# Sums of weights from the first down projection on, and seven products for four blocks of the second batch

## The chip, the cores and the metric

The kernel runs on one core of one Trainium2 chip. The metric is the device time of one execution in microseconds (us). Of the core's engines the page names PE (TensorE, matrix products), PEld (its weight loads), DVE (VectorE), ACT (ScalarE), POOL (GpSimd) and SP (SyncE, which only issues DMAs here). PE writes its results to eight banks of PSUM; ACT and DVE carry them from there to SBUF. Each engine works through its own queue in order, so an instruction that waits holds up everything queued behind it.

## What is computed

Attention in a causal window of 128 positions with a linear bias for each head, for 8 batches of 8 heads with 576 positions and 64 channels, and after it a bilinear layer on the 4608 tokens (512 channels, 1536 hidden units):

```python
scores = scale * np.matmul(q, k.transpose(0, 1, 3, 2))
mask = (rel >= 0) & (rel < window)
scores = np.where(mask, scores + bias[None], -1000000000.0)
attn = np.exp(scores - np.max(scores, axis=-1, keepdims=True))
attn = attn / (np.sum(attn, axis=-1, keepdims=True) + 1e-09)
x = np.matmul(attn, v)              # then laid out as (tokens, 512)
out = (x @ w_a) * (x @ w_b) @ w_out
```

All of it is float32. The kernel gets that accuracy on PE from pairs of float16 numbers: a value is split into a high part and a remainder, and a product is made of three float16 products (high by high, high by low, low by high).

## The kernel before, in words

The work goes by batch, 0 to 7. For each batch stand an **up** stage (both products with `w_a` and `w_b` and their elementwise product, giving the hidden tile `h`) and a **down** stage (the product with `w_out`). PE's queue is written out by hand from batch 1 on: `batch(b)` walks through `up` and then `down` and, at each step of these generators, lets `attention()` advance in proportion (`Pace.along`). So the attention of the next batch lies between the matmuls of this one. An item of `attention()` is one pair of heads; batch 1's up stage carries 2.85 items (from place 5.15 to 8), its down stage two, and every later up and down stage two each. The order on DVE, ACT and POOL is made by a scheduler from the order of the code and priorities; SP's is that of the code. In batch 0 the scheduler also places PE's instructions.

The hidden units are 12 blocks `f` of 128. For one block the tokens of a batch make two halves (`t`) and the 512 channels two halves, and there are two ways to make the block:

- **plain** (`first_up`, `up_plain`): 4 results of 12 matmuls, 48 matmuls of 128x288 in all. They read the four parts of `wup[:, f]` and the splits 0, 1, 2 and 7 (`B12`) of the tokens in `xs`. ACT copies two results (L867) and casts the product (L848); DVE makes two products (L869) and the remainder (L849).
- **fast** (`up_fast`): 7 results of 6 matmuls, 42 in all, after a scheme of Strassen's kind. It needs sums of the parts of the weights (three in `wsum[:, f]`, the fourth written over part 3 of `wup[:, f]`, so that the block cannot be plain afterwards) and sums of the parts of the tokens (splits 3 to 6 in `xs`). Carrying away is ACT L881, L893, L899, L848; DVE L888, L904, L909, L916, L849; POOL L911. Two blocks run beside each other in two lanes, after four steps in which the first lane runs alone. Two of a block's products add to the bank that ACT L881 has just copied from.

`ways` says for each batch which blocks are plain and which fast; plain blocks come first. The sums of the weights come from the generator `sums_of_weights`, `spread`: 25 steps, one for each block and half of the channels, the last only finishing. A step adds on POOL (L248 on 512 columns, L249 to L252 on 128 each), and a step later the result is split by two casts on ACT (L258) and two subtractions on DVE (L260). `quota` says in which steps of a stage how many of them are handed out. POOL's part is ordered behind the last `bias` (L365, the row of biases of an attention item), ACT's behind the last evacuation of a result. The space for the intermediate sums is the end of `wsum` for blocks 0 to 7 and the attention's rotating tile `t` for blocks 8 to 11.

The weights themselves are converted before, in `weights` (the last of it in batch 0's down stage, with L231 on ACT and L232 on DVE writing `wdn`). The tokens are split by `split_x(st, plain, fast)` when a batch's attention is done, which is in the down stage of the batch before: each split is a cast on ACT (L441) and a subtraction on DVE (L442); the fast way adds four subtractions on POOL (L455, L458, L460, L465), which write over the tokens in `v`. The next `v` is loaded by SP once that tile is free.

The lines that matter most, besides those that follow below:

```python
def split(n, src):
    act.copy(xs[:, n, 0, :, :], src)
    vec.tensor_tensor(out=xs[:, n, 1, :, :], in0=src, in1=xs[:, n, 0, :, :], op=ALU.subtract)

# split_x(st, plain, fast), in short
split(0, b11)
if plain:
    split(1, b21); split(2, b22); split(B12, b12)
if not fast:
    return
# then four subtractions on POOL, and splits 4, 6, 5, 3 (and 2, 1 where not plain)
```

Of the kernel before, what the change touches and what calls it, by code (L numbers as in the profile page):

```python
# [21 lines left out]
B, H, S, D = 8, 8, 576, 64  # L22
# [24 lines left out]
def attention_then_bilinear_ffn(ctx: ExitStack, tc: tile.TileContext, qT, kT, vP, w_a, w_b, w_out, rel, slopes2, outT):  # L47
# [392 lines left out]
# [4 lines that stand above are left out]
    def split_x(st, plain, fast):  # L444

        b11, b12, b21, b22 = (st.v[:, k:k + 2, t:t + HT] for k in (0, 2) for t in (0, HT))
        split(0, b11)
        if plain:
            split(1, b21)
            split(2, b22)  # L450
            split(B12, b12)
        if not fast:
            return
        yield
        pool.tensor_tensor(out=b11, in0=b12, in1=b11, op=ALU.subtract)  # L455
        if not plain:
            split(2, b22)
        pool.tensor_tensor(out=b12, in0=b22, in1=b12, op=ALU.subtract)  # L458
        split(4, b11)
        pool.tensor_tensor(out=b22, in0=b22, in1=b11, op=ALU.subtract)  # L460
        yield
        if not plain:
            split(1, b21)
        split(6, b12)
        pool.tensor_tensor(out=b21, in0=b21, in1=b22, op=ALU.subtract)  # L465
        yield
        split(5, b22)
        split(3, b21)
        yield
# [197 lines left out]
    def attention():  # L667
# [29 lines left out]
        st, prev = load_v(1), None  # L697
# [4 lines left out]
        for i in range(n + 1):  # L702
            b, p = 1 + i // NPAIR, i % NPAIR
# [6 lines left out]
            if p == 1 and b > 1:  # L710
                st = load_v(b)
# [44 lines left out]
            if prev and p == 0:  # L756
                states[b - 1] = st
                assert started["down"] == b - 2
                for k, _ in enumerate(split_x(st, b - 1 <= 3, b - 1 >= 2)):
                    yield i + (4.2 + 0.2 * k) / 7  # L760
            yield i + 5 / 7
            if o:
# [198 lines left out]
    def out_scale(st):  # L961

        oi = small.tile([P, 1], F32, tag="oi", name="oi")
        vec.tensor_scalar(out=oi, in0=st.g, scalar1=smin, scalar2=so, op0=ALU.mult, op1=ALU.mult)
        vec.tensor_scalar(out=oi, in0=oi, scalar1=st.sv, scalar2=st.sv, op0=ALU.mult, op1=ALU.mult)
        vec.reciprocal(oi, oi)
        return oi

    def weave(main, *sides):

        for n, _ in enumerate(main):
            for side, a, z, steps in sides:
                if a <= n < z:
                    for _ in range((n + 1 - a) * steps // (z - a) - (n - a) * steps // (z - a)):
                        next(side, None)
# [24 lines left out]
    weights = chain(up_weights(), down_weights())  # L1000
# [4 lines left out]
    h = hid.tile([P, NF, 2, 2, HT], F16, name="h")  # L1005
# [4 lines left out]


    every = list(range(NF))
    ways = [(every, [])] * 2 + [(every[6:], every[:6]), (every[10:], every[:10])] + [([], every)] * (B - 4)
    att = Pace(attention())
    spread = sums_of_weights()

    quota = [((), ()), (((8, 48, 9),), ((0, 48, 4),)), (((0, 24, 3),), ((0, 48, 5),)), ((), ((0, 48, 4),))] + [((), ())] * (B - 4)

    def first_batch():
        st = states[0]  # L1020
        weave(att.along(first_up(st, h), 49, 3.2), (weights, 0, 40, 50))
        weave(att.along(first_down(0, out_scale(st), h), 24, 5.15), (weights, 0, 12, 12))
        for _ in weights:
            pass

# [8 lines left out]
    with tc.manual_schedule(engines=SP):  # L1034
        first_batch()
# [45 lines left out]
```

## Time and profile before

| | |
|---|---|
| median of 3 runs | 991.28 us (991.03 to 994.67) |
| the profiled execution's own time | 989.81 us |
| its span, first to last instruction | 988.0 us |
| granted TensorE clock, mean | 0.995 |
| DVE, ACT, POOL busy | 669.0, 635.6, 255.3 us |
| DMA packets | 102.82 MB, mean 104 GB/s |

The profile's page shows one execution. A row of a group gives line, engine and operation, what it writes and reads with the shapes, how often, then the busy time and the mean ns of one, and last the idle time of the engine before it with what ended it. The view by stretches of time gives for each stretch its length, then for each engine the busy time with the number of its instructions, and last PE's granted clock and the DMA share. The view of one tile gives for each group the shortest, the median and the longest duration. Stretches are cut here where PE passes from one stage to the next by the timeline: batch 0's up and down stages begin at 55.9 and 153.5 us, batch 1's at 200.3 and 281.8, batch 2's at 324.1 and 400.0, batch 3's at 441.1 and 513.2, batch 4's at 554.8 and 626.4, batch 5's at 667.1 and 737.9; the last up and down stages begin at 887.4 and 949.3.

### The profile page before, as it was taken

The numbers are of one execution on the slowest core, as the hardware profiler recorded it, in microseconds if no ns is written. First come the engines' busy times: TensorE is split into PE (matmuls) and PEld (weight loads), VectorE is DVE, ScalarE is ACT, GpSimd is POOL, SyncE is SP. The second block draws the span as 40 slices with busy tenths as digits, with TensorE's granted clock in tenths as the row PEclk, the third lists the DMA queues.
The fourth block names the chain that finished last, engine by engine and source line by source line (L and its number), as shares of the span: only waits on it lengthen the run. The fifth ranks groups of instructions, "written<-read, shape, count | busy, mean of one in ns | idle before, by whom it ended". The sixth has DMA issues, their size and how long they took to land.

```text
span 988.0 us, 23867 instructions
## 1 busy us (share of the span) xinstructions
PE 962.1 (97%) x9339; PEld 748.9 (76%) x9339; DVE 669.0 (68%) x1867; ACT 635.6 (64%) x1729; POOL 255.3 (26%) x309
## 2 busy tenths in 40 slices
PE   7899999999999999999999999999999999999998
PEld 5567777677777777777777777777777777877776
DVE  5979998668688657777778677757776576514520
ACT  5977769667676667766767766777667766413321
POOL 1211122032546313541225222211232012311100
PEclk8999999999999999999999999999999999999999
DMA  8434753664337234463345362373245432200001
GB/s 333 168 126 172 231 154 67 151 158 92 80 74 183 68 69 87 107 172 75 68 92 121 120 118 65 87 191 84 59 84 117 133 74 38 55 34 5 1 13 36
DMA packets 148432, 102.82 MB, mean 104 GB/s; under 512 B 120032, under 2 KB 128352, under 8 KB 147296
## 3 DMA queue, kind: packets, MB, share of 16 engines
q1 hardware_dynamic: 138816, 91.77, 38.2%
q10 hardware_dynamic: 9504, 9.54, 3.0%
q8 instruction: 73, 1.20, 0.5%
q14 instruction: 39, 0.32, 0.1%
HBM read 48.33 MB, written 9.44 MB: 58 GB/s over the span
## 4 chain that ended last, share of the span: by engine, by line
PE 69%; DVE 12%; ACT 7%; DMA 7%; issue 3%; POOL 1%; SPq 0%; ACTq 0%; DVEq 0%
PE ch L856 19%; PE dn_ps L952 18%; PE p L856 14%; PE up_ps L856 9%; PE x_ps L507 4%; DMA v<-in_vP 4%; PE sc_ps L384 3%; DVE phl L406 2%; PE dn_ps L818 2%; ACT t L389 1%; DVE wsum L135 1%; DVE xs L442 1%; ACT phl L405 1%; DVE wsum L134 1%; DMA qk<-in_kT 1%
## 5 line engine op out<-in xcount | busy, mean ns | idle before, releaser
L856 PEld LDWEIGHTS <-wup 128*128 128x128 f16 x3072 | 296.3, 98 | 82.0 <-issue 5.7
L952 PE MATMUL dn_ps<-h,wdn 128*128 128x288 f16 x2016 | 254.4, 286 | 0.0
L952 PEld LDWEIGHTS <-wdn 128*128 128x128 f16 x2016 | 193.9, 98 | 52.0 <-issue 0.2
L856 PE MATMUL up_ps<-xs,wup 128*128 128x288 f16 x1536 | 194.6, 286 | 1.1 <-ACT rc L867 0.8
L856 PEld LDWEIGHTS <-wsum 128*128 128x128 f16 x1152 | 111.7, 98 | 32.0 <-issue 2.5
L911 POOL TENSOR_TENSOR rc<-rc,row 128x288 f32<-128x288 f32 x64 | 62.3, 974 | 279.8 <-DVE row L909 263.9
L389 ACT ACTIVATE t<-t,mn 128x192 f32<-128x192 f32 (+2 forms) x252 | 107.2, 427 | 24.5 <-DVE mn L388 24.4
L856 PE MATMUL ch<-xs,wup 128*128 128x288 f16 x768 | 115.0, 286 | 0.5 <-ACT row L893 0.5
L856 PE MATMUL p<-xs,wup 128*128 128x288 f16 x768 | 115.1, 286 | 0.0
L406 DVE SCALAR_TENSOR_TENSOR phl<-t,rin,phl 128x192 f16<-128x192 f32 (+2 forms) x252 | 104.6, 454 | 15.3 <-ACT phl L405 15.1
L856 PE MATMUL ch<-xs,wsum 128*128 128x288 f16 x768 | 111.5, 286 | 1.1 <-ACT rc L881 1.1
L848 ACT CAST h<-rc 128x576 f16<-128x576 f32 x96 | 64.1, 668 | 69.1 <-DVE rc L916 37.2
L405 ACT ACTIVATE phl<-t,rin 128x192 f16<-128x192 f32 (+2 forms) x252 | 88.9, 425 | 25.3 <-DMA pT<-phl 12.7
L849 DVE TENSOR_TENSOR h<-rc,h 128x576 f16<-128x576 f32 x90 | 69.5, 772 | 30.5 <-ACT h L848 29.7
L388 DVE CUSTOM_DVE_ANT_0 t<-sc_ps,bias,neg 128x192 f32<-128x192 f32 (+2 forms) x216 | 73.9, 389 | 7.6 <-PE sc_ps L384 7.5
L957 ACT ACTIVATE row<-dn_ps,oi 128x288 f32<-128x288 f32 x56 | 27.6, 493 | 55.9 <-PE dn_ps L952 55.9
L893 ACT ACTIVATE row<-ch,g 128x288 f32<-128x288 f32 x64 | 31.8, 497 | 48.9 <-PE ch L856 48.9
L442 DVE TENSOR_TENSOR xs<-v,xs 128x576 f16<-128x576 f32 x52 | 47.8, 935 | 21.4 <-ACT xs L441 21.3
L888 DVE TENSOR_TENSOR rc<-p,rc 128x288 f32<-128x288 f32 x64 | 29.1, 454 | 44.3 <-PE p L856 34.7
L365 POOL TENSOR_SCALAR bias<-rel_sb,ninv,sl_sb 128x192 f32<-128x192 f32 x24 | 20.0, 832 | 147.8 <-DVE mn L388 129.8
L856 PE MATMUL p<-xs,wsum 128*128 128x288 f16 x384 | 57.5, 286 | 0.0
L436 POOL TENSOR_TENSOR xq<-xq,sq 128x576 bf16<-128x576 bf16 x22 | 29.2, 1325 | 75.7 <-ACT sq L435 75.7
(155 smaller groups left out, 1386.1 us busy)
## 6 DMA issues: line engine op xcount, KB each, us to landing
v<-in_vP SPq DMA_DIRECT2D x8, 1280.0 KB, 6.2
out<-row ACTq DMA_DIRECT2D x62, 144.0 KB, 1.8
qk<-in_qT SPq DMA_DIRECT2D x28, 288.0 KB, 4.0
qk<-in_kT SPq DMA_DIRECT2D x28, 288.0 KB, 4.4
wdn<-in_w_a SPq DMA_DIRECT2D x12, 512.0 KB, 5.1
wdn<-in_w_b SPq DMA_DIRECT2D x12, 512.0 KB, 6.1
wdn<-in_w_out SPq DMA_DIRECT2D x12, 512.0 KB, 4.6
qst<-qkh SPq DMA_DIRECT2D x24, 144.0 KB, 2.7
```

Source lines behind the costliest of these rows:

```text
L388: vec.tensor_tensor_reduce(out=t[:, c:c + w], in0=ps[:, c:c + w], in1=o.bias[:, WIN - w:WIN], scale=-0.125 if o.b == 1 else o.neg, scalar= ...
L389: act.activation(t[:, c:c + w], t[:, c:c + w], AF.Exp, bias=o.mn[:, n:n + 1], scale=-1.0, accum_out=o.sm[:, n:n + 1])
L405: act.activation(phl[:, 0, pc:pc + w], e, AF.Copy, scale=s)
L406: vec.scalar_tensor_tensor(out=phl[:, 1, pc:pc + w], in0=e, scalar=s, in1=phl[:, 0, pc:pc + w], op0=ALU.mult, op1=ALU.subtract)
L442: vec.tensor_tensor(out=xs[:, n, 1, :, :], in0=src, in1=xs[:, n, 0, :, :], op=ALU.subtract)
L507: last = pe.matmul(xp[oc // 512][64 * h:64 * h + 64, o0:o0 + w], vt[0:rows, c:c + 64], probs(pt, rows, blocks, h), start=(n == 0 and first ...
L848: act.copy(h[:, f, :, 0, :], hid)
L849: eng.tensor_tensor(out=h[:, f, :, 1, :], in0=hid, in1=h[:, f, :, 0, :], op=ALU.subtract)
L856: pe.matmul(ps[:, 0:HT], w[:, wi, k, :], xs[:, b, xi, k, :], start=(first and n == 0), stop=(last and n == len(ks) - 1), skip_group_check= ...
L893: last_read[0] = last_main[0] = act.activation(mid, ch, AF.Copy, scale=st.g)
L911: pool.tensor_tensor(out=x0, in0=x0, in1=mid, op=ALU.mult)
L952: pe.matmul(ps[:, 0:HT], wdn[:, f, wi, e * P:(e + 1) * P], h[:, f, t, hi, :], start=(m == 0 and n == 0), stop=(m == NF - 1 and n == 2))
```

## The change

```diff
-                for k, _ in enumerate(split_x(st, b - 1 <= 3, b - 1 >= 2)):
+                for k, _ in enumerate(split_x(st, b - 1 <= 1, b - 1 >= 1)):
...
-    ways = [(every, [])] * 2 + [(every[6:], every[:6]), (every[10:], every[:10])] + [([], every)] * (B - 4)
+    ways = [(every, []), (every[4:], every[:4])] + [([], every)] * (B - 2)
...
-    quota = [((), ()), (((8, 48, 9),), ((0, 48, 4),)), (((0, 24, 3),), ((0, 48, 5),)), ((), ((0, 48, 4),))] + [((), ())] * (B - 4)
+    quota = [((), ()), (((8, 60, 10),), ((0, 48, 6),))] + [((), ())] * (B - 2)
...
-        weave(att.along(first_down(0, out_scale(st), h), 24, 5.15), (weights, 0, 12, 12))
+        weave(att.along(first_down(0, out_scale(st), h), 24, 5.15), (weights, 0, 12, 12), (spread, 12, 24, 9))
```

In `ways` the plain blocks go from 12, 12, 6, 2, 0, ... to 12, 8, 0, 0, ...: batch 1 makes blocks 4 to 11 plain and then 0 to 3 fast, and batches 2 and 3 make all 12 fast. The 25 steps of the sums were handed out in batch 1 (9 up, 4 down), batch 2 (3 and 5) and batch 3's down stage (4); now 9 go to the second half of batch 0's down stage, 10 to batch 1's up and 6 to its down stage. The tokens of batch 1 get all eight splits instead of four, those of batches 2 and 3 seven instead of eight. On PE the program has 17,411 rows instead of 17,555: 72 matmuls and 72 weight loads fewer.

The order of the program shows where the sums now stand. First POOL, in batch 0's down stage, where `bias` belongs to an attention item, `xq` to the squares of the tokens and `wsum` to the sums. Before, three biases pass and the sums begin behind the third:

```order
L365 TENSOR_SCALAR bias<-rel_sb,ninv,sl_sb 128x192
L436 TENSOR_TENSOR xq<-xq,sq 128x576
L365 TENSOR_SCALAR bias<-rel_sb,ninv,sl_sb 128x192 x2
L248 TENSOR_TENSOR wsum<-wup 128x512 x3
```

In the changed program three steps of the sums stand right behind the first of these biases, and two of the four subtractions of the tokens in `v` and the next bias behind those:

```order
L365 TENSOR_SCALAR bias<-rel_sb,ninv,sl_sb 128x192
L248 TENSOR_TENSOR wsum<-wup 128x512 x3
...
L251 TENSOR_TENSOR wsum<-wsum 128x128 x3
L252 TENSOR_TENSOR wsum<-wsum 128x128 x3
L458 TENSOR_TENSOR v<-v 128x2x288
L436 TENSOR_TENSOR xq<-xq,sq 128x576
L365 TENSOR_SCALAR bias<-rel_sb,ninv,sl_sb 128x192
L248 TENSOR_TENSOR wsum<-wup 128x512 x3
L460 TENSOR_TENSOR v<-v 128x2x288
```

Of the nine steps three stand ahead of the second bias and six behind it. Next ACT, where batch 0's down stage passes into batch 1's up stage. `up_ps` is the first result of that stage, and `t` and `sm` are the exponentials of the attention. Before:

```order
L389 ACTIVATE t,sm<-t,mn 128x192 x3
L401 ACTIVATE rin<-sm 128x5
L826 DMA out<-row 128x288
L405 ACTIVATE phl<-t,rin 128x64
L405 ACTIVATE phl<-t,rin 128x128
L405 ACTIVATE phl<-t,rin 128x192 x3
L867 COPY rc<-up_ps 128x288
```

In the changed program casts of the sums (L258) and of two more splits (L441) stand among them; each waits for POOL:

```order
L441 CAST xs<-v 128x576
L258 CAST wup<-wsum 128x128 x3
L389 ACTIVATE t,sm<-t,mn 128x64
L389 ACTIVATE t,sm<-t,mn 128x128
L389 ACTIVATE t,sm<-t,mn 128x192
L441 CAST xs<-v 128x576
L389 ACTIVATE t,sm<-t,mn 128x192 x2
L826 DMA out<-row 128x288
L258 CAST wsum<-wsum 128x3x128
L401 ACTIVATE rin<-sm 128x5
L867 COPY rc<-up_ps 128x288
L258 CAST wsum<-wsum 128x3x128 x2
```

The first copy of `up_ps` now stands ahead of the five `phl` and behind a cast of the sums. Last DVE, in the four fast blocks of batch 1: `ch` and `p` are the banks of the seven products, `both` and `cl` belong to the scale of the next item's queries and keys. In the changed program:

```order
L329 TENSOR_SCALAR both<-halves,qs 128x2
L904 TENSOR_TENSOR rc<-ch,rc 128x288
L260 TENSOR_TENSOR wup<-wsum,wup 128x128
L260 TENSOR_TENSOR wsum<-wsum 128x3x128
L909 SCALAR_TENSOR_TENSOR row<-p_3749,g,row 128x288
L916 SCALAR_TENSOR_TENSOR rc<-rc,g,ch 128x288
L260 TENSOR_TENSOR wup<-wsum,wup 128x128
L260 TENSOR_TENSOR wsum<-wsum 128x3x128
L904 TENSOR_TENSOR rc<-ch,rc 128x288
L402 RECIPROCAL rin<-rin 128x5
L849 TENSOR_TENSOR h<-rc,h 128x2x288
```

Before, plain blocks stood there, with one evacuation (L869) and one remainder (L849) between the same work of the attention and of the sums:

```order
L869 SCALAR_TENSOR_TENSOR rc<-rc,g,up_ps 128x288
L402 RECIPROCAL rin<-rin 128x5
L849 TENSOR_TENSOR h<-rc,h 128x2x288
L406 SCALAR_TENSOR_TENSOR phl<-t,rin,phl 128x64
L406 SCALAR_TENSOR_TENSOR phl<-t,rin,phl 128x128
L406 SCALAR_TENSOR_TENSOR phl<-t,rin,phl 128x192 x3
L869 SCALAR_TENSOR_TENSOR rc<-rc,g,up_ps 128x288
L260 TENSOR_TENSOR wup<-wsum,wup 128x128
L260 TENSOR_TENSOR wsum<-wsum 128x3x128
```

What moved is that the evacuations of four fast blocks now stand in this place, among the same work of the attention and of the sums.

## The prediction

> **What bounds the kernel now.** I begin with the page's head and its busy line.
>
> ```profile
> span 988.0 us, 23867 instructions
> PE 962.1 (97%) x9339; PEld 748.9 (76%) x9339; DVE 669.0 (68%) x1867; ACT 635.6 (64%) x1729; POOL 255.3 (26%) x309
> ```
>
> PE is busy for 97% of the span. A busy PE need not be at its peak, so I look in the chain of waits for long runs of matmuls without a break.
>
> ```profile
> 325.70 0.79 PE sc_ps L384 x20
> ...
> 326.67 13.25 PE up_ps L856 x108
> ...
> 949.44 35.29 PE dn_ps L952 x288
> ```
>
> 288 matmuls take 35.29 us, 122.5 ns each, and 108 of an up stage take 13.25 us, 122.7 ns. This is the price of a matmul of 288 columns when nothing holds PE; 20 of the scores take 0.79 us. Whether it is held is read by stages; the columns are length, then busy time and number for PE, PEld, DVE, ACT and POOL.
>
> ```profile
> core 0: us, PE busy (x) PEld busy (x) DVE busy (x) ACT busy (x) POOL busy (x), PEclk, DMA share, GB/s
> 55.90:153.50 97.60, 93.54 (x894) 70.81 (x893) 88.56 (x214) 69.31 (x174) 18.85 (x24) 1.00 0.52 168
> 153.50:200.30 46.80, 44.37 (x458) 33.85 (x456) 31.21 (x97) 33.38 (x91) 6.13 (x6) 1.00 0.60 125
> 200.30:281.80 81.50, 80.25 (x799) 63.27 (x798) 61.10 (x176) 59.44 (x172) 38.11 (x56) 1.00 0.47 105
> 281.80:324.10 42.30, 41.13 (x409) 31.89 (x408) 33.18 (x98) 30.36 (x90) 20.74 (x23) 1.00 0.61 146
> 324.10:400.00 75.90, 74.96 (x747) 59.16 (x745) 52.54 (x144) 50.88 (x136) 18.57 (x25) 1.00 0.30 65
> 400.00:441.10 41.10, 40.86 (x408) 31.83 (x406) 30.98 (x96) 29.34 (x88) 21.32 (x27) 1.00 0.67 159
> 441.10:513.20 72.10, 71.89 (x723) 56.78 (x721) 52.17 (x146) 50.90 (x137) 17.57 (x19) 1.00 0.37 76
> 513.20:554.80 41.60, 40.87 (x409) 31.81 (x406) 30.58 (x96) 29.51 (x89) 19.04 (x22) 1.00 0.60 150
> 554.80:626.40 71.60, 71.14 (x711) 55.58 (x709) 52.58 (x149) 50.71 (x135) 16.31 (x16) 1.00 0.37 75
> 626.40:667.10 40.70, 40.70 (x408) 31.91 (x407) 25.45 (x93) 29.05 (x87) 8.72 (x7) 1.00 0.62 157
> 667.10:737.90 70.80, 70.80 (x711) 55.59 (x709) 50.88 (x144) 48.95 (x130) 16.32 (x16) 1.00 0.35 74
> 887.40:949.30 61.90, 61.90 (x507) 49.31 (x505) 30.23 (x58) 22.40 (x48) 8.73 (x11) 1.00 0.01 4
> ```
>
> From batch 1 on no stage leaves PE idle for over 1.25 us; DVE and ACT stand at 60 to 80%. So a matmul left out should shorten the span by its full price, wherever its engines can still carry the results away. The waits of PE that matter below are single ones (us in total, times, longest):
>
> ```profile
> PE wtot L103 <- DVE c L102: 2.4, 1, 2.4
> ...
> PE qtot L337 <- DVE both L329: 1.4, 2, 1.2
> ...
> PE ch L856 <- ACT rc L881: 1.1, 4, 0.4
> ```
>
> **The change, part by part. The matmuls.** Plain blocks fall from 32 to 20, as the group of `up_ps` counts them: 1536 matmuls are 32 blocks of 48. Twelve blocks become fast and lose 6 matmuls each, 72 in all.
>
> ```profile
> L856 PE MATMUL up_ps<-xs,wup 128*128 128x288 f16 x1536 | 194.6, 286 | 1.1 <-ACT rc L867 0.8 <-DVE v L628 0.3
> ```
>
> 72 times 122.5 ns is 8.82 us: batch 1 gives 24 matmuls (2.94 us), batch 2 gives 36 (4.41), batch 3 gives 12 (1.47).
>
> **Batches 2 and 3** become what batches 4 and 5 already are, so their stages can be read instead of summed. The up stage of batch 2 goes from 75.9 to the 71.6 of batch 4, minus 4.3 us; its down stage from 41.1 to 40.7, minus 0.4, because no sums are left there (DVE 30.98 us against 25.45). Batch 3's up stage goes from 72.1 to between 71.6 and 70.8, minus 0.9, and its down stage from 41.6 to 40.7, minus 0.9. Together minus 6.5 us; the matmuls alone would make 5.9. The one split fewer in each batch lies in these same rows.
>
> **Batch 1** has no row of its kind. Its matmuls give minus 2.94. Against this stands work on the other engines that moves there or to batch 0's down stage. The price of a step of the sums is read from the view of the tile `wsum` (shortest, median and longest ns):
>
> ```profile
> L248 POOL TENSOR_TENSOR wsum<-wup x16: 1149/1160/1667, 213.1 to 357.1; 128x512 f32<-128x512 f16 x16
> L249 POOL TENSOR_TENSOR wsum<-wsum x16: 452/484/1041, 217.0 to 358.4; 128x128 f32<-128x128 f32 x16
> L250 POOL TENSOR_TENSOR wsum<-wsum x16: 451/520/987, 217.4 to 358.8; 128x128 f32<-128x128 f32 x16
> L251 POOL TENSOR_TENSOR wsum<-wsum x16: 451/456/766, 219.9 to 359.7; 128x128 f32<-128x128 f32 x16
> L252 POOL TENSOR_TENSOR wsum<-wsum x16: 448/457/1080, 221.2 to 360.4; 128x128 f32<-128x128 f32 x16
> L258 ACT CAST wup<-wsum x16: 286/298/302, 230.3 to 406.0; 128x128 f16<-128x128 f32 x16
> L258 ACT CAST wsum<-wsum x16: 510/512/514, 230.5 to 406.2; 128x384 f16<-128x384 f32 x16
> L260 DVE TENSOR_TENSOR wup<-wsum,wup x16: 277/292/1279, 230.8 to 406.3; 128x128 f16<-128x128 f32 x16
> L260 DVE TENSOR_TENSOR wsum<-wsum x16: 544/558/1503, 231.1 to 406.7; 128x384 f16<-128x384 f32 x16
> ```
>
> By the medians a step is 3.08 us of POOL (5.54 by the longest), 0.81 of ACT and 0.85 of DVE. The splits are priced by their groups:
>
> ```profile
> L442 DVE TENSOR_TENSOR xs<-v,xs 128x576 f16<-128x576 f32 x52 | 47.8, 935 | 21.4 <-ACT xs L441 21.3
> L441 ACT CAST xs<-v 128x576 f16<-128x576 f32 x52 | 34.0, 668 | 17.4 <-POOL v L460 8.6 <-POOL v L465 3.2 <-DVE v L628 3.1
> L460 POOL TENSOR_TENSOR v<-v 128x576 f32<-128x576 f32 x6 | 9.1, 1512 | 0.8 <-DVE xs L442 0.8
> ```
>
> *Batch 0's down stage* gets eight finished sums and four splits: DVE 8 x 0.85 + 4 x 0.935 = 10.5 us, ACT 8 x 0.81 + 4 x 0.668 = 9.2, POOL 9 x 3.08 + 4 x 1.5 = 34. With its row's 31.21 and 33.38 DVE would have 41.7 and ACT 42.6 us of work in 46.8, even if nothing slid into batch 1. PE's order here is unchanged, and the fast blocks come only after eight plain ones (384 matmuls, 47 us), so the sums themselves are not late. The four added splits also hold `v` longer, and with it SP's load of batch 2's `v` and the rows queued behind it; its squares stand a dozen rows later on ACT. I take 0.3 us of added waiting; the ends are nothing and the 6.3 us that POOL would cost at its slowest, worked out below, and the medians are nearer to nothing.
>
> *The start of the fast blocks* costs a wait for L881, since the first lane runs alone: at most 0.4 us by the row above. Batch 1 now has it too: 0.4.
>
> *The crowd in the fast blocks.* They take 28 of the stage's 60 steps, so 28/60 of the 2.85 items of attention, 1.33, lie beside 168 matmuls. What an item of an up stage costs is the difference of the rows at 667.1 (two items) and at 887.4 (none), halved: PE 4.45 us, DVE 10.3, ACT 13.3. PE then has 168 x 0.1225 + 1.33 x 4.45 = 26.5 us. Four blocks' evacuation is a third of the row at 887.4: DVE 10.1, ACT 7.5. Attention adds 13.7 and 17.7, and 28/52 of ten steps of the sums 4.6 and 4.4. DVE gets 28.4 us and ACT 29.6 us in 26.5. So ACT has 3.1 us too much, and work must slide into the down stage behind, where DVE and ACT have some 9 and 12 us free (row at 281.8), less 1.7 for each by the two more steps there. Sliding costs PE nothing unless a matmul waits for it; the first that may are `qtot` and the scores of the next item. The price lies between nothing and 3.1 us. The nearest row with a nearly full DVE is 55.9:153.5, at 91% over 97.6 us with PE idle 4.06; its longest wait there, 2.4 us, is the one-off total of the weights. I take 1.0.
>
> **Sum.** -6.5 - 2.94 + 0.3 + 0.4 + 1.0 = -7.7 us. The profiled execution took 989.81 us and becomes 982.1. The median of the runs shown is 991.28, 1.5 us above it, and becomes **983.5**.
>
> **Rivals.** *No crowding.* Work slides without any matmul noticing: -6.5 - 2.94 = -9.4, so 981.9. For it: PE was idle only 1.25 us in batch 1's up stage at 75% DVE, and in the plain part an item of attention now has 21 steps (60 by 2.85) instead of 17. Against it: each down stage with sums lost 0.2 to 1.2 us.
>
> *The crowd in full.* The 3.1 us are paid, and 1.3 more for one wait of the kind of `qtot` (1.2 at most above) at the switch: -6.5 - 2.94 + 0.4 + 3.1 + 1.3 + 0.3 = -4.3, so 987.0. For it: the two engines' queues are in order, and an `L881` that stands behind five `phl` holds a bank.
>
> *POOL holds ACT at the start of batch 1, and the kernel gets slower.* The casts of the second three sums now stand on ACT ahead of the second L867 copy, and wait for POOL. POOL's queue there, and the ACT rows behind those casts, from the timelines:
>
> ```profile
> 172.36 0.50 POOL L365 TENSOR_SCALAR bias<-rel_sb,ninv,sl_sb 128x192 f32<-128x192 f32 x1
> 187.95 0.69 ACT L420 ACTIVATE v<-x_ps 128x512 f32<-128x512 f32 x2
> 192.65 0.50 POOL L365 TENSOR_SCALAR bias<-rel_sb,ninv,sl_sb 128x192 f32<-128x192 f32 x1 [1.47 <-DVE mn L388]
> ...
> 204.73 1.68 ACT L405 ACTIVATE phl<-t,rin 128x64 f16<-128x64 f32 x5 [0.45 <-DMA pT<-phl]
> 206.31 0.38 ACT L867 COPY rc<-up_ps 128x288 f32<-128x288 f32 x1
> ...
> 209.14 1.24 ACT L343 ACTIVATE qkh<-qk,own 128x1152 f16<-128x1152 f32 x1
> ```
>
> The first three sums start at 172.9 and end, at 3.08 us a step, at 182.1; POOL's next instruction needs the tokens that ACT copies by 188.6, so it idles. The second three start at about 193.2 and with two subtractions of 1.5 us end at 205.4. Behind that stand a cast, five `phl`, a `qkh` and the second L867: 0.5 + 1.68 + 1.24 + 0.38 = 3.8 us, to 209.2. PE needs that bank, the third of five, at its eighth result: 200.3 plus 7 x 12 x 0.1225 plus 0.6 for 16 scores, 211.2. So 2.0 us are to spare, and this costs nothing at 3.08 us. With s us a step the wait is 3s - 15.7 (first three, once s is above 5.2) plus 3 (s - 3.08) less 2.0. It takes away all 7.7 us at s = 5.8, and at twice the median, 6.16, it is 10.0 us: 993.5, slower than before. At the longest of each row, 5.54, it is 6.3. For it: the longest of L249, L250 and L252 are twice the median already. Against it: all five would have to be slow in every step, and the median shows that most are not.
>
> [...]
>
> *The change does not do what it says.* The order has 72 matmuls fewer and the fast blocks in place, so only the way in which the stages would fail to shorten is left, which the rivals above cover.
>
> **How the numbers follow.** The forecast 983.5 gets 0.60, no crowding (981.9) 0.15, the crowd in full (987.0) 0.18, POOL holding ACT (990 to 993.5) 0.05; 0.02 stay for what I did not see. The range runs from 981.0, no crowding with a run's scatter of about a us, to 988.5, the crowd in full with the same; POOL's rival lies outside. A measurement of this kernel can tell about 0.5%, 5 us, from no change; the bound is 986.3. The forecast and the case without crowding lie below it, the crowd in full about half and half: faster 0.83, within 0.5% 0.14, slower 0.03.
>
> **What would show it.** In the new profile 960 matmuls of `up_ps` instead of 1536; up stages of batches 2 and 3 of 71 to 72 us and down stages below 41; batch 1 in all some 122 us instead of 123.8, with PE waits of about 1 us in its fast blocks and the `qtot` behind them; the first down stage within 0.5 us of its 46.8. The prediction is wrong if PE waits over 2 us at one place in batch 1: for L881 or `qtot`, it is the crowd; for L867 at its start, with ACT waiting for L252, it is POOL; or if a step of the sums takes POOL much over 3.3 us.

## The result, and the profile after

The changed kernel takes 1003.28 us (median of six runs, 1002.81 to 1004.78) where the kernel before took 992.03 (988.85 to 994.67) beside it: the ratio is 1.0116, 95% interval 1.0096 to 1.0136. It is 11 us slower; 7.7 us less were forecast.

The head of the page and its busy line, and PE's group of plain blocks:

```profile
span 1002.7 us, 23805 instructions
PE 965.1 (96%) x9267; PEld 747.3 (75%) x9267; DVE 685.0 (68%) x1893; ACT 642.5 (64%) x1743; POOL 279.1 (28%) x325
```

```profile
L856 PE MATMUL up_ps<-xs,wup 128*128 128x288 f16 x960 | 125.9, 290 | 4.4 <-DVE rc L869 3.2
```

The 960 matmuls are there and PE has 72 instructions fewer, yet its busy time rose by 3 us, and the span has 11.7 us more without PE. The rows by stages, in the same columns as before: batch 0's down stage, batch 1's eight plain and its four fast blocks, its down stage, then batch 2's and batch 3's two stages.

```profile
156.90:208.10 51.20, 46.11 (x458) 34.95 (x456) 40.90 (x104) 35.29 (x98) 27.48 (x31) 0.97 0.51 108
208.10:266.30 58.20, 54.02 (x487) 41.40 (x486) 48.47 (x127) 39.98 (x118) 31.39 (x44) 0.97 0.43 101
266.30:301.00 34.70, 27.07 (x292) 20.55 (x290) 29.62 (x70) 25.51 (x72) 27.23 (x36) 0.98 0.36 69
301.00:343.80 42.80, 41.88 (x407) 32.23 (x406) 34.22 (x102) 29.90 (x90) 27.36 (x35) 0.98 0.59 143
343.80:416.70 72.90, 71.42 (x711) 55.71 (x709) 52.84 (x150) 51.94 (x139) 17.58 (x19) 1.00 0.39 82
416.70:457.40 40.70, 40.70 (x408) 31.91 (x407) 24.56 (x90) 27.77 (x83) 8.72 (x7) 1.00 0.61 153
457.40:529.40 72.00, 71.12 (x711) 55.57 (x709) 51.86 (x147) 50.25 (x133) 16.34 (x16) 1.00 0.35 74
529.40:570.10 40.70, 40.70 (x408) 31.91 (x407) 24.57 (x90) 27.95 (x84) 8.73 (x7) 1.00 0.66 146
```

Batches 2 and 3 come near the forecast: their four stages take 226.3 us where 230.7 stood, 4.4 less, where 6.5 less were forecast; most of what is missing is batch 2's up stage, 72.9 us instead of 71.6. The loss is ahead of them: 51.2 us where 46.8 stood, and batch 1's up stage takes 58.2 + 34.7 = 92.9 where it took 81.5. In the fast blocks PE works 27 of 34.7 us, and neither DVE nor ACT is full. The granted clock, 1.00 before, is 0.97 to 0.98 in the four rows ahead of batch 2. Of the 14.7 us between the spans of the two profiled executions 3.4 lie ahead of batch 0's down stage, and they are chance: the first up stage took 99.7 us here and 97.6 before, and 97.2 to 98.3 in e3 to e8 and e10 below, which have the same four fast blocks and splits. PE's longest waits after the first stage (total, times, longest):

```profile
PE x_ps L507 <- DMA pT<-phl: 4.9, 1, 4.9
PE ch L856 <- DVE rc L904: 3.3, 1, 3.3
PE up_ps L856 <- DVE rc L869: 3.2, 2, 2.1
...
PE ch L856 <- ACT rc L881: 2.4, 2, 2.0
PE sc_ps L384 <- DVE mn L388: 2.2, 1, 2.2
```

Before, only the first of these stood above 2 us. I follow three of them back.

**The wait for pT in batch 0's down stage.** `pT` is the transposed copy of `phl`, which DVE's L406 finishes. The timeline of DVE and POOL there, of the kernel before and of the changed one (start, length, how many):

```profile
173.13 1.46 DVE L406 SCALAR_TENSOR_TENSOR phl<-t,rin,phl 128x192 f16<-128x192 f32 x4 [0.52 <-ACT phl L405]
```

```profile
176.56 4.05 DVE L406 SCALAR_TENSOR_TENSOR phl<-t,rin,phl 128x192 f16<-128x192 f32 x4 [0.52 <-ACT phl L405]
...
176.25 3.61 POOL L248 TENSOR_TENSOR wsum<-wup 128x512 f32<-128x512 f16 x3
179.81 0.58 POOL L249 TENSOR_TENSOR wsum<-wsum 128x128 f32<-128x128 f32 x1
```

The same four rows take 4.05 us instead of 1.46, and they lie beside the first three sums on POOL. PE waits for what these rows deliver, in the timelines before and after:

```profile
183.93 1.54 PE L507 MATMUL x_ps<-pT,vhl 128*64 128x128 f16 x42 [2.44 <-DMA pT<-phl]
```

```profile
190.17 2.77 PE L507 MATMUL x_ps<-pT,vhl 128*64 128x128 f16 x42 [4.90 <-DMA pT<-phl]
```

The wait grew by 2.46 us, and the same 42 matmuls then took 2.77 us instead of 1.54: they ran at half clock (granted 0.50 from 190.17 us to 192.95, 1.00 before at 183.93 to 185.47). Not all of the growth is from these four rows: with them back at 1.46 us (e4 below) the wait is still 3.6.

**Two waits in the fast blocks.** The wait for L881 at 267.6, and the one for L904 at 296.0, each with what stands ahead on POOL, DVE and ACT:

```profile
264.37 3.81 POOL L248 TENSOR_TENSOR wsum<-wup 128x512 f32<-128x512 f16 x3
...
266.54 1.85 DVE L406 SCALAR_TENSOR_TENSOR phl<-t,rin,phl 128x192 f16<-128x192 f32 x2 [0.52 <-ACT phl L405]
268.32 0.50 DVE L869 SCALAR_TENSOR_TENSOR rc<-rc,g,up_ps 128x288 f32<-128x288 f32 x1
...
268.85 0.67 ACT L848 CAST h<-rc 128x576 f16<-128x576 f32 x1 [2.00 <-DVE rc L869]
269.43 0.39 ACT L881 COPY rc<-ch 128x288 f32<-128x288 f32 x1
```

```profile
295.95 1.45 POOL L455 TENSOR_TENSOR v<-v 128x576 f32<-128x576 f32 x1
...
296.06 1.75 DVE L260 TENSOR_TENSOR wsum<-ws,wsum 128x384 f16<-128x384 f32 x1
297.74 0.50 DVE L916 SCALAR_TENSOR_TENSOR rc<-rc,g,ch 128x288 f32<-128x288 f32 x1
298.16 0.99 DVE L406 SCALAR_TENSOR_TENSOR phl<-t,rin,phl 128x192 f16<-128x192 f32 x2
299.08 0.45 DVE L904 TENSOR_TENSOR rc<-ch,rc 128x288 f32<-128x288 f32 x1
```

In the first, two `phl` rows that end with POOL's third L248 hold the last plain block's L869, that holds ACT's cast L848, and behind the cast stands the copy L881 that frees PE's bank. In the second, an L260 of 1.75 us (median 0.56 before) begins with POOL's L455 and outlasts it, and L904 comes late. From 291.8 us to L904 DVE works without a pause there, and its rows run over by 2.8 us in that time, against the 3.3 that PE waits.

**How general that is.** I counted DVE's rows with two inputs in SBUF (`phl`, `qkl`, `vhl`, `h`, `xs`, `wup`, `wsum`) that start while a POOL instruction with two inputs (TENSOR_TENSOR) runs and at least 150 ns before it ends: 98 in the changed kernel, and 84 of them run over the usual length of their form (which a quarter of its rows do not exceed) by more than 100 ns. In the kernel before it is 76 of 84. Of DVE's scores, reciprocals and PSUM products in the changed kernel it is 1 of 125. Every row between 157 and 344 us that runs over lies beside a POOL instruction; together they run over by 9.5, 9.2, 8.1 and 7.0 us in the four stretches, where the kernel before has 1.5 (batch 0's down stage), 7.5 and 7.3 (batch 1's stages).

The prediction reckoned with slow rows on POOL alone; what these counts show is slow rows on DVE. Why rows that lie side by side run over, no run shows.

### The profile page after: what moved, and what is told of

Read it like the earlier page. It is cut to its first block, busy times and chain, and to the rows that moved or that the text cites. A ratio compares the mean times of both kernels' runs of the same rounds, so it can differ in the third digit from the quotient of the medians.

```text
span 1002.7 us, 23805 instructions
## 1 busy us (share of the span) xinstructions
PE 965.1 (96%) x9267; PEld 747.3 (75%) x9267; DVE 685.0 (68%) x1893; ACT 642.5 (64%) x1743; POOL 279.1 (28%) x325
## 4 chain that ended last, share of the span: by engine, by line
PE 71%; DVE 10%; ACT 7%; DMA 7%; issue 2%; POOL 2%; SPq 0%; ACTq 0%; DVEq 0%; POOLq 0%
PE ch L856 21%; PE dn_ps L952 16%; PE p L856 15%; PE up_ps L856 9%; PE x_ps L507 4%; DMA pT<-phl 3%; PE sc_ps L384 2%; DVE phl L406 2%; ACT t L389 2%; DMA v<-in_vP 1%; PE dn_ps L818 1%; PE sc_ps L380 1%; DMA qk<-in_kT 1%; DVE xs L442 1%; ACT phl L405 1%
## 5 line engine op out<-in xcount | busy, mean ns | idle before, releaser
L856 PEld LDWEIGHTS <-wup 128*128 128x128 f16 x2784 | 269.7, 98 | 83.1 <-issue 12.4
L856 PEld LDWEIGHTS <-wsum 128*128 128x128 f16 x1368 | 132.9, 98 | 43.1 <-issue 7.9
L911 POOL TENSOR_TENSOR rc<-rc,row 128x288 f32<-128x288 f32 x76 | 74.1, 974 | 324.5 <-DVE row L909 305.1
L856 PE MATMUL ch<-xs,wsum 128*128 128x288 f16 x912 | 133.6, 287 | 5.9 <-DVE rc L904 3.3
L856 PE MATMUL ch<-xs,wup 128*128 128x288 f16 x912 | 136.6, 286 | 1.6 <-ACT row L893 1.3
L856 PE MATMUL p<-xs,wup 128*128 128x288 f16 x912 | 136.7, 286 | 0.0
L856 PE MATMUL up_ps<-xs,wup 128*128 128x288 f16 x960 | 125.9, 290 | 4.4 <-DVE rc L869 3.2
L406 DVE SCALAR_TENSOR_TENSOR phl<-t,rin,phl 128x192 f16<-128x192 f32 (+2 forms) x252 | 105.3, 460 | 18.4 <-ACT phl L405 18.3
L848 ACT CAST h<-rc 128x576 f16<-128x576 f32 x96 | 64.1, 668 | 68.5 <-DVE rc L916 37.6
L849 DVE TENSOR_TENSOR h<-rc,h 128x576 f16<-128x576 f32 x90 | 68.6, 762 | 24.4 <-ACT h L848 23.6
L893 ACT ACTIVATE row<-ch,g 128x288 f32<-128x288 f32 x76 | 37.9, 499 | 64.6 <-PE ch L856 64.6
L388 DVE CUSTOM_DVE_ANT_0 t<-sc_ps,bias,neg 128x192 f32<-128x192 f32 (+2 forms) x216 | 73.8, 388 | 2.9 <-PE sc_ps L384 2.6
L856 PE MATMUL p<-xs,wsum 128*128 128x288 f16 x456 | 68.4, 286 | 0.0
L888 DVE TENSOR_TENSOR rc<-p,rc 128x288 f32<-128x288 f32 x76 | 34.5, 454 | 46.9 <-PE p L856 31.8
L916 DVE SCALAR_TENSOR_TENSOR rc<-rc,g,ch 128x288 f32<-128x288 f32 x76 | 38.7, 510 | 24.5 <-PE ch L856 24.4
```

The lines of the kernel that those rows point to most:

```text
L388: vec.tensor_tensor_reduce(out=t[:, c:c + w], in0=ps[:, c:c + w], in1=o.bias[:, WIN - w:WIN], scale=-0.125 if o.b == 1 else o.neg, scalar= ...
L406: vec.scalar_tensor_tensor(out=phl[:, 1, pc:pc + w], in0=e, scalar=s, in1=phl[:, 0, pc:pc + w], op0=ALU.mult, op1=ALU.subtract)
L848: act.copy(h[:, f, :, 0, :], hid)
L849: eng.tensor_tensor(out=h[:, f, :, 1, :], in0=hid, in1=h[:, f, :, 0, :], op=ALU.subtract)
L856: pe.matmul(ps[:, 0:HT], w[:, wi, k, :], xs[:, b, xi, k, :], start=(first and n == 0), stop=(last and n == len(ks) - 1), skip_group_check= ...
L911: pool.tensor_tensor(out=x0, in0=x0, in1=mid, op=ALU.mult)
```

## The experiments

Theory P: POOL's additions for the sums, packed into the stretch from batch 0's down stage to batch 1's end, block DVE's two-input rows; what these deliver comes late, PE waits, and after a long wait runs at half clock for a while (in the changed kernel for 3.41 us behind waits of 4.9, 2.1 and 3.3 us). Rivals: the crowd of the four fast blocks alone (C), the load and order of ACT's and DVE's queues (Q), the added splits (S). Kernels e4 to e6, e8, e9 and e11 leave sums out of the computation.

**One part of the change at a time.**

```diff
# e1: batch 1 plain, without the four added splits; quota (8,48,10), (0,48,6)
-    ways = [(every, []), (every[4:], every[:4])] + [([], every)] * (B - 2)
+    ways = [(every, [])] * 2 + [([], every)] * (B - 2)
# e2: as e1, and no sums in first_down; quota (8,48,13), (0,48,12)
```

> Batch 1 stays plain (32 blocks fewer than before only in batches 2 and 3), the sums keep their nine early steps in batch 0's down stage. Theory P (the early sums on POOL slow VectorE's instructions in batch 0's down stage and at the start of batch 1, PE waits for what these deliver and then runs some 3.4 us at half clock after each long wait): that loss, about 4.4 us in the down stage and 4.4 in the eight plain blocks behind it, stays, the 8 us of the four fast blocks go, the 6 us gained in batches 2 and 3 stay: about 994 to 996 us. Theory C (all of the loss is the crowd of the four fast blocks, and the rest is scatter): 985 to 987 us.

> No sums in batch 0's down stage, batch 1 plain, all 25 steps of the sums in batch 1 (13 in its up stage, 12 in its down stage), batches 2 and 3 by seven products. Theory P and theory C both: batch 0 and the start of batch 1 as in the kernel before, batches 2 and 3 shorter by 6 us, at most 2 us back in batch 1's down stage, where twelve steps replace four: 986 to 988 us, faster than before. If neither holds (batches 2 and 3 by seven products lose elsewhere): 991 or more.

e1 gave 993.88 us, ratio 1.0022 (1.0011 to 1.0034): next to theory P's figure, not C's; batch 0's down stage stayed at 52.0 us with a wait of 5.0 for `pT`. (Its sums write over a weight that batch 1's plain blocks still read, and PE waits 1.5 and 0.3 us there for L258 and L260.) e2 gave 999.05, ratio 1.0076 (1.0052 to 1.0101), where both theories had said 986 to 988. Batch 0's down stage was back at 46.5, but batch 1 took 86.6 + 45.5 and batch 2's up stage 76.4; DVE's overruns there were 13.6, 11.5 and 5.3 us, and PE waited 4.3 us for one L388. So it is not the early place alone that is dear. From here on theory P has a second half, D: the additions are dear because they are packed; spread over batches 1 to 3, as before, they hide.

**POOL's additions left out.**

```diff
# e4: the five additions only from the tenth step on; e5: zeros written instead
+                if 2 * f + k >= 9:
# e6: none at all; both halves of a step then split a constant
+                z = halves[:, 0:1].unsqueeze(2).to_broadcast([P, 4, P])
```

> The changed kernel without the five POOL additions of the first nine steps of the sums (these sums are left out of the computation; ScalarE and VectorE still make their casts and subtractions of what lies there). Theory P: the phl rows of VectorE in batch 0's down stage go back from 4 us to 1.5 us, the wait for pT from 4.9 to about 2.4 us, and some 8 us of the loss are gone: 993 to 996 us. Rival Q (the added casts, subtractions and splits fill ScalarE's and VectorE's queues, POOL itself does no harm): within 2 us of the changed kernel, 1001 to 1004 us.

> As the kernel before this one in the list, but POOL writes zeros to the same places instead of adding (45 instructions that write SBUF and read none of it; the first nine sums are left out of the computation). If it is POOL's reading beside VectorE's two inputs that blocks: like the kernel without the additions, 993 to 996 us, with phl rows of 1.5 us. If POOL's being busy (what is queued behind on it: biases, differences of the tokens) or its writing is what counts: nearer to the changed kernel, 999 to 1004 us.

> The changed kernel without the POOL additions of all 24 steps (left out of the computation; ScalarE and VectorE still make each step's two casts and two subtractions, of a constant). Theory P (POOL's additions block VectorE rows that start beside them): VectorE's overrun rows in the four fast blocks, 8.1 us in the changed kernel, fall below 3, the fast stretch from 34.7 us to 27 to 30, batch 1's down stage to 41.5, and the whole to 989 to 992 us. Rival Q (the order and load of ScalarE's and VectorE's queues holds PE in the fast blocks, POOL does not): the stretch stays 33 to 35 us and the whole 996 to 998, as without the first nine steps' additions.

e4 gave 997.34 (ratio 1.0057, 1.0034 to 1.008), e5 998.17 (1.0057, 1.0034 to 1.0081), e6 990.57 (0.9995, 0.998 to 1.001). In e4 and e5 the four `phl` rows were back at 1.46 us, and the plain stretch fell to 54.5 and 52.9 us, but the fast stretch stayed at 34.7 and 35.6 with its waits of about 2 (twice) and 3.3 us: its additions were still there. The times of e4 and e5 lie above P's 993 to 996, and P's wait of 2.4 us for `pT` did not come: it was 3.6 in e4 and 4.6 in e5, and batch 0's down stage took 49.4 and 50.5 us. The memsets, which read nothing, cost no more in all than leaving the additions out; they are shorter, though (4.4 us for nine of 512 columns). e6's stages (batch 0's down stage, the fast blocks, batch 1's down stage):

```profile
153.60:202.70 49.10, 46.18 (x458) 34.66 (x457) 40.05 (x111) 40.23 (x111) 14.96 (x10) 0.97 0.53 114
...
257.30:287.20 29.90, 26.19 (x292) 20.30 (x290) 24.33 (x71) 23.80 (x69) 7.50 (x7) 1.00 0.42 80
287.20:328.70 41.50, 40.91 (x409) 31.84 (x407) 28.28 (x100) 30.21 (x91) 9.28 (x7) 1.00 0.61 148
```

The fast stretch is 29.9 us, as P said, and Q's 33 to 35 fall. DVE's overruns in the four stretches are 5.2, 0.2, 2.6 and 2.0 us, where the changed kernel has 9.5, 9.2, 8.1 and 7.0. DVE's groups over the same two stages, of the changed kernel and of e6 (there L406 is L400 and L260 is L254; busy us, mean ns):

```profile
L406 DVE SCALAR_TENSOR_TENSOR phl<-t,rin,phl 128x192 f16<-128x192 f32 x37 | 23.7, 690 | 1.6 <-ACT phl L405 1.6
L260 DVE TENSOR_TENSOR wsum<-wsum 128x384 f16<-128x384 f32 x16 | 12.5, 784 | 0.7 <-ACT wsum L258 0.5
```

```profile
L400 DVE SCALAR_TENSOR_TENSOR phl<-t,rin,phl 128x192 f16<-128x192 f32 x37 | 15.1, 456 | 1.8 <-ACT phl L399 1.7
L254 DVE TENSOR_TENSOR wsum<-halves,wsum 128x384 f16<-128x384 f32 x18 | 11.1, 618 | 0.4
```

Thirty-seven `phl` rows of one shape take 690 ns each with the additions and 456 without them. What e6 prices is the additions with all that hangs on them: without them the casts do not wait for POOL either, and the scheduler orders ACT's and DVE's rows somewhat differently (in the three stages, 280 of some 333 rows of DVE keep their order). No run separates these from the held rows.

**The sums moved, or left out wholly.**

```diff
# e7: no step beside the fast blocks
+    quota = [((), ()), (((8, 32, 6),), ((0, 48, 10),))] + [((), ())] * (B - 2)
# e3: none in batch 0's down stage
+    quota = [((), ()), (((0, 26, 9), (26, 60, 8)), ((0, 48, 8),))] + [((), ())] * (B - 2)
# e8, e9, e11: sums_of_weights only yields; other weights are read instead
-        w = wup[:, a[0], a[1]] if a[1] < 4 else wsum[:, a[0], a[1] - 4]
+        w = wup[:, a[0], a[1]] if a[1] < 4 else wup[:, a[0], a[1] - 4]
```

> The changed kernel with no step of the sums beside batch 1's four fast blocks: six steps beside its eight plain blocks, ten in its down stage. Theory P: the fast stretch falls from 34.7 us to 28 to 30, the down stage behind loses 1 to 3 us and the plain stretch 0 to 2 by the steps that move there: 998 to 1001 us. Rival Q (four fast blocks beside attention are too much for ScalarE and VectorE by themselves): the stretch stays over 33 us and the whole 1003 or more.

> The changed kernel with no sums in batch 0's down stage: nine steps beside the eight plain blocks' first 26 pieces, eight beside the rest of batch 1's up stage, eight in its down stage. Theory D: batch 0's down stage falls to 49 us (splits alone), but the same 25 steps in less time cost as much in batch 1: 1001 to 1006 us. If batch 0's down stage is the bad place: 994 to 998 us.

> The changed kernel without any work of the sums (all 24 steps are left out of the computation, the fast blocks multiply by other weights of the same shape): four fast blocks in batch 1 and the splits moved into batch 0's down stage remain. Theory P: batch 0's down stage 47 us, the plain stretch 53 to 54, the fast stretch 27 to 28, 983 to 986 us. If the fast blocks or the splits by themselves cost PE (rival Q, and a rival S for the splits): the fast stretch over 32 us, or batch 0's down stage over 49, 988 us or more.

> The kernel without any work of the sums (all 24 steps left out of the computation, the fast blocks multiply by other weights of the same shape) once more, now with batch 1 plain, so without the fast operands' four splits and four subtractions in batch 0's down stage. Rival S (these splits and subtractions cost PE there: 49.3 us with them and no sums, 46.9 in the kernel before): batch 0's down stage 46.5 to 47.2 us, the wait for pT 2.6 us or less instead of 3.7, and 985 to 987 us. If they cost nothing: the down stage stays at 49 us and the whole at 989 or more.

> The kernel before without any work of the sums (all 24 steps left out of the computation, the fast blocks multiply by other weights of the same shape), its blocks as they are. Theory D (the sums are dear where they are packed; spread over batches 1 to 3 they hide): 989 to 991 us, less than 2 us below the kernel before. If each step has a price of its own (14 us for 24): 977 to 980 us.

e7 gave 1000.18 (1.0102, 1.0071 to 1.0133): the fast stretch fell to 29.9 us as P said, and the loss came back in the plain stretch (59.3), the down stage (43.2) and batch 2 (75.9). e3 gave 1003.02 (1.0125, 1.0106 to 1.0145): batch 0's down stage at 49.2, batch 1 at 58.1 + 33.4 + 46.9. Against the same blocks without sums (e8 and e9, next), the 25 steps cost 8.4 us in e1, 11.9 in e7, 13.3 in the changed kernel, 13.8 in e2 and 14.2 in e3, each to some 2 to 3 us: least where batch 1 is plain and they lie in three stages, and everywhere more than in the kernel before.

Without the sums' work the changed kernel (e8) took 988.52, ratio 0.9982 (0.9969 to 0.9994), not the 983 to 986 of theory P; the kernel before (e11) 987.16, ratio 0.9963 (0.9949 to 0.9978), between theory D's figure and the other, nearer to D's. So the 24 steps cost the kernel before 0.37% (3.7 us, 0.15 a step) and the changed one 1.16 + 0.18 = 1.34% (13.3 us, 0.55 a step). With batch 1 plain as well (e9) it is 984.86, 0.9937 (0.9915 to 0.9959). The rows of e8 and e9: batch 0's down stage, batch 1's up stage (in e8 in two rows), and in e9 its down stage and batch 2's up stage:

```profile
153.60:202.90 49.30, 45.83 (x458) 34.92 (x456) 37.49 (x101) 35.83 (x96) 14.35 (x10) 0.97 0.52 115
202.90:256.00 53.10, 51.87 (x487) 40.60 (x486) 33.02 (x110) 34.22 (x99) 2.20 (x2) 1.00 0.46 108
256.00:285.00 29.00, 26.17 (x292) 20.33 (x290) 20.51 (x59) 19.97 (x56) 8.24 (x7) 1.00 0.44 83
```

```profile
153.90:201.00 47.10, 44.66 (x459) 33.85 (x458) 31.26 (x97) 33.64 (x92) 6.13 (x6) 1.00 0.60 126
201.00:282.50 81.50, 80.28 (x800) 63.34 (x798) 50.29 (x162) 54.66 (x155) 5.79 (x6) 1.00 0.49 108
282.50:323.20 40.70, 40.70 (x408) 31.91 (x407) 24.36 (x89) 28.57 (x86) 7.55 (x6) 1.00 0.54 137
323.20:394.40 71.20, 70.94 (x710) 55.59 (x708) 51.28 (x146) 49.44 (x131) 16.32 (x16) 1.00 0.37 77
```

Two things follow. Rival S holds beside P: with the added splits and no sums batch 0's down stage takes 49.3 us, without them 47.1. (Beside the sums the splits add nothing: e1, which lacks them, took 52.0.) How, the timelines of e8 and e9 show (in both L457 is L455, L851 is L849, L408 is L406):

```profile
165.56 1.79 POOL L457 TENSOR_TENSOR v<-v 128x576 f32<-128x576 f32 x1 [1.82 <-DVE xs L444]
167.32 2.39 POOL L851 TENSOR_TENSOR h<-rc,h 128x576 f16<-128x576 f32 x1
...
168.50 2.55 DVE L408 SCALAR_TENSOR_TENSOR phl<-t,rin,phl 128x64 f16<-128x64 f32 x5
```

```profile
166.21 1.28 POOL L851 TENSOR_TENSOR h<-rc,h 128x576 f16<-128x576 f32 x1 [1.89 <-ACT h L850]
...
168.66 1.53 DVE L408 SCALAR_TENSOR_TENSOR phl<-t,rin,phl 128x64 f16<-128x64 f32 x5
```

The moved subtraction makes POOL's last remainder of batch 0 late, and that then meets `phl`. And four fast blocks in batch 1 gain nothing even without sums: 53.1 + 29.0 = 82.1 us against 81.5 for twelve plain ones. PE idles 4.1 us there instead of 1.2, which takes back what the 24 matmuls save (2.94); 2.4 us of it are two waits, for L388 and L904 by the changed kernel's lines.

**The half clock.**

```diff
# e10: ahead of the last wsum product of block 3, for batch 1 alone
+        if f == 3 and fills.pop():
+            pf = ps_ef.tile([P, 512], F32, tag="ef", name="pf")[:, 0:HT]
+            for _ in range(26):
+                pe.matmul(pf, wup[:, 0, 0, 0, 0, :], xs[:, 0, 0, 0, :], start=True, stop=True, skip_group_check=True)
```

> The changed kernel with 26 matmuls more, which nobody reads, ahead of the matmul that waits 3.48 us for VectorE's L904 at the end of batch 1's fast blocks; they take 3.2 us of PE's time, all of it in that wait. Theory K (a window in which PE idles halves the granted clock for the next 3.4 us, 1.7 us lost each time): the piece at half clock that begins at 299.4 us in the changed kernel's profile is gone, the matmuls behind run at 122 ns instead of 240, and the whole is 1 to 2 us shorter than the changed kernel: 1001 to 1002.5 us. Rival (the half clock does not follow PE's idling): the piece stays and the time is 1003 or more.

The product behind the wait and the first of the down stage, in the changed kernel and in e10:

```profile
299.57 1.60 PE L856 MATMUL ch<-xs,wsum 128*128 128x288 f16 x6 [3.32 <-DVE rc L904]
300.97 1.64 PE L952 MATMUL dn_ps<-h,wdn 128*128 128x288 f16 x6
```

```profile
297.19 0.90 PE L856 MATMUL ch<-xs,wsum 128*128 128x288 f16 x6
297.93 0.90 PE L958 MATMUL dn_ps<-h,wdn 128*128 128x288 f16 x6
```

The half clock behind that wait is gone, and batch 1's down stage is 1.3 us shorter (41.5). The whole is not: 1003.62 us, ratio 1.0137 (1.011 to 1.0165). In its profiled run another wait of 2.1 us, with a piece at half clock behind it, appeared at 455 us. So the local effect is shown, and one of it is too small to be told in the total.

**Ways out that failed.** k3 and k4 make the five additions on DVE (`vec.tensor_tensor` for `pool.tensor_tensor`), in the changed kernel and in the one before; k1 makes batch 3 wholly fast, k5 eight blocks of batch 2, both from the kernel before and with some steps of the sums moved ahead for it.

> The changed kernel with the five additions of each step of the sums on VectorE instead of POOL (some 1.4 us of VectorE a step, 33 us in all). Theory P: without POOL's instructions beside them VectorE's rows no longer overrun (some 20 us less), so the added load nearly cancels and the time lies between that without the additions, 990.6, and the changed kernel's: 992 to 998 us. If VectorE's load rather than the blocking were the cause, it gets worse: over 1003.

> The kernel before with the same edit (additions of the sums on VectorE; its schedule of sums and blocks is kept). Theory P: its stages with sums, where VectorE stands at 75%, lose less to blocking than they gain in load or the reverse by little: 988 to 992 us. If it is slower than 994, VectorE's load there was nearer to its limit than its busy share shows.

> The kernel before with batch 3 wholly by seven products: two blocks more, and the last four steps of the sums moved from batch 3's down stage into batch 2 (two beside its fast blocks, seven in its down stage instead of five). Theory P: 12 matmuls less (1.5 us) and up to 1.5 us less in batch 3, against at most 1 us in batch 2: 989 to 991 us where the kernel before has 991.5, within 0.5% of it. If the steps moved cost PE as much as those moved to batch 1: 992 to 995.

> The kernel before with eight instead of six blocks of batch 2 by seven products (12 matmuls less, 1.5 us) and the sums as far ahead as these need: 11 and 5 steps in batch 1 instead of 9 and 4, 2 and 3 in batch 2 instead of 3 and 5. Theory D: three more steps in batch 1 cost 0 to 2 us: 990 to 992 us, the same as before. If it comes out at 989.5 or less, the way of the change is right and only its amount was too much; if over 993, even this many steps are too many.

k3 gave 1010.86 (1.0207, 1.0179 to 1.0235), against theory P's 992 to 998: the overruns fell (to 5.3, 2.5 and 3.5 us in the three stretches), but a step took DVE 2.0 us instead of 1.4, the scheduler's order changed with it, DVE had 47 us of work in the 52 from 157 to 209 us, and PE then waited 10.2 us in one place of the plain stretch. So DVE's own load, or the other order, is a second limit; the run doesn't tell which. k4 gave 996.41 (1.0059, 1.0033 to 1.0085), k1 993.10 (1.0017, 0.9998 to 1.0037), k5 994.61 (1.0035, 1.0022 to 1.0049). All three were expected at 992 us or less; k5 lost 3.5 us with three more steps of the sums in batch 1, where its 12 matmuls fewer were to win 1.5. No version that computes everything was faster than the kernel before.

## Why the prediction was wrong, point by point

The step that failed is the price of the sums of weights: they stand in the forecast with 0.3 us of waiting in batch 0's down stage and a part of the 1.0 us of the crowd, and they cost 13.3 us, 9.6 more than in the kernel before. Taking the ratios of the runs times 991 us, four steps lead from the kernel before to the changed one, each known to 1.5 to 2.6 us. Without the sums' work the kernel before gains 3.7 us (e11). From there batches 2 and 3, made wholly by seven products, gain 2.6 (e9). Four fast blocks of batch 1 with their splits lose 4.5 (e8). The sums, packed as in the change, lose 13.3: 12.0 with POOL's additions (from e6 to the changed kernel) and 1.3 with their casts and subtractions (from e8 to e6). -3.7 - 2.6 + 4.5 + 13.3 = +11.5, where -7.7 were forecast.

The parts do not simply add. With batch 1 plain the sums cost 8.4 us (from e9 to e1), beside four fast blocks 13.3 (from e8 to the changed kernel). So about 5 us, known to some 3.5, belong to the two together.

- **The matmuls, and batches 2 and 3**: the number of matmuls is right. Reading stages that already exist was good, though the profile shows 4.4 us of the 6.5.
- **Batch 0's down stage, +0.3**: it became 4.4 longer. The step reads "the medians are nearer to nothing". I looked at the lengths of POOL's rows alone, where the median of L248, 1160 ns, is next to the shortest, 1149, and priced only what POOL would be late by. The queue that PE waits for is DVE's. Its `phl` rows were in the trace of before with both lengths (47 of 128x192 from 153.5 to 324.1 us, 418 ns in the median and 1554 the longest), and nine in ten of all two-input rows there that met a two-input instruction of POOL ran over (76 of 84); I had not looked. Nor were the splits priced beyond a share of this waiting; alone, without the sums, they make 2.2 us (from e9 to e8).
- **The crowd, +1.0**: the stretch was to take 26.5 us plus 1.4 and took 34.7. Its loads were nearly right (DVE 29.6 us against 28.4, ACT 25.5 against 29.6). But sums of load take queues as if they could slide freely; 8.1 of DVE's 29.6 us were overruns, at places where PE had a bank to wait for. And without the sums it is still 29.0. The sign named for being wrong came, a wait of over 2 us at one place in batch 1, but at L869, L388 and L904, which the prediction had not named.
- **The rival of POOL holding ACT** had the right engine and the wrong victim: PE's wait for L867 was 0.9 us, those for DVE 8.7 in all. I gave it 0.05, from a point of decision (a step of 5.8 us on POOL) that a loss by POOL's sums doesn't need: three steps took POOL 8.8 us at 176, 2.9 each, while DVE lost 2.6 us in one group. ACT did wait for POOL's sums, 3.8 us at two casts L258, but only in batch 1's down stage, where PE's longest wait was 0.7.
- **What no term had: the clock.** In the changed kernel's profile, after the start of the first up stage, PE has 240 ns instead of 122 for a matmul in four pieces of its record of the granted clock, of 3.41 us (the first of 6.83), that begin at 149.2, 190.1, 224.3 and 299.4 us, within or just behind waits; in the kernel before's profile there is none between 29 us and the end. The first lies in batch 0's up stage, behind a wait that the kernel before has too (2.4 us for `wtot`), so it is not of the change. At half clock the other 10.2 us are 5.1 lost at most. The pieces come and go from run to run: over the 68 runs of the kernel before beside the experiments the time falls by 0.39 us for each 0.001 of mean granted clock, and from its mean there, 0.992, to the changed kernel's 0.986 that makes some 2.3 us. This is a correlation, not a test. The length of a wait does not settle it: the piece at 224.3 followed one of 2.1 us, while the wait of 2.44 for `pT` in the kernel before left the clock at full, as did those of 2.0 for L881 and 2.2 for L388 in the changed one. So theory K holds for the one wait that e10 filled, and not for every wait; what else decides, and what makes the pieces 3.41 us long, no run shows.

What stays open: how the 12 us of the additions divide between held rows, casts that wait, the changed order and the half clock behind the waits, and why so few more steps in one place decide it: e2, with 25 steps in batch 1 where the kernel before has 13, pays 1.39% for them (1.0076 against e9's 0.9937), 13.8 us, where the kernel before pays 3.7.

## What to carry to other kernels

Before work is moved to an idle engine, look in the trace for rows of the *other* engines that lie beside its instructions, and compare their lengths with and without that neighbour (690 ns against 456 here); the mover's own rows may look unharmed (2.9 us a step here, against 3.08 by the medians before). Work that nearly hides when spread (0.15 us a step here) need not hide when packed (0.55), and a table of busy shares doesn't show where it stops, because queues are in order: here PE waited 2.0 us for the copy L881, which stood on ACT behind a cast that itself waited 2.0 us for DVE. And a wait of PE can cost beyond itself, in the clock behind it: 240 ns a matmul instead of 122 for 3.41 us behind waits of 4.9, 2.1 and 3.3 us, though not behind those of 2.0 and 2.2.

## What the runs showed of the hardware that I had not expected

DVE's rows with two SBUF inputs were held by POOL's two-input instructions nearly always (84 of 98 in the changed kernel), but hardly by POOL's one-input `bias` row (2 of the 20 that met no other row of POOL's), though that reads SBUF too, and none of the five that met a memset in e5 was held. Some rows of DVE with a single input were held as well: small `TENSOR_SCALAR`s of 1 to 4 columns (15 of 36 beside POOL's two-input instructions), and once by a `bias` row and memsets, in e5:

```profile
175.14 0.50 POOL L371 TENSOR_SCALAR bias<-rel_sb,ninv,sl_sb 128x192 f32<-128x192 f32 x1
175.34 1.72 DVE L404 TENSOR_SCALAR rin<-sm 128x4 f32<-128x4 f32 x1 [0.78 <-ACT t L395]
...
175.59 1.45 POOL L256 MEMSET wsum<- 128x512 f32 x3
```

Six of this line's eight rows in e5 take 0.15 to 0.17 us; this one took 1.72 and ended with the third memset. The `phl` rows that `pT` needs stand behind it, and e5 is the run in which the wait for `pT` stayed at 4.6 us with `phl` rows of 1.46. So leaving out the reads is no cure for every neighbour.
